# A fused attention and MLP-mixer kernel: prologue by head pairs, casting loads, column-tiled sums, and a transpose by transfer

## Chip, cores, metric

One core of one Trainium2 chip. The metric is the device time of one execution in microseconds (us). The kernel before took 424.72 us (median of 3 runs, 424.33 to 428.24) when it was first measured.

## The reference

Sliding-window attention with eight global positions, then an MLP mixer over tokens and over channels. Inputs are f32; B=8, H=8, S=576, D=64.

```python
# mask: |i-j| <= 32, or i global, or j global (8 global positions)
scores = (q @ k.T) / 8;  scores[~mask] = -1e9
attn = softmax(scores);  x = (attn @ v) as [B, 576, 512]
h  = relu(x.T @ w_tok1) @ w_tok2          # over tokens, 576 -> 256 -> 576
u  = x + h.T
out = u + relu(u @ w_ch1) @ w_ch2         # over channels, 512 -> 1536 -> 512
```

## The kernel before

Each batch has a *sparse* list of steps (transposes `T`, scores `S_`, global rows `GK`, global sums `OG`, attention times v `PV`, token mixing `M1`, `M2`, the turn of u `M3`) and a *dense* list (channel mixing `M4`, `M5`, about two thirds of TensorE's work). The dense list of batch b is merged with the sparse list of batch b+1 in proportion to given weights. Batch 0's sparse list has nothing to overlap with: it is the prologue. Batch 7's dense list is the tail. In the traces each engine works through a list of its own, and an instruction that waits holds up those behind it in this list: in the changed kernel a 0.32 us copy of POOL began at 44.19 us, behind a cast that had waited 19.12 us for its load. The list is not always in the order in which the steps are written, because steps can be moved when the program is built. So the orders below are read from traces, not from the source.

```python
def load(b):                                  # f32, tile by tile, SyncE queue
    for ti, ten in enumerate((q, k)):
        for t in range(NT):
            nc.sync.dma_start(out=n32[ti][0:n, t], in_=ten[b, :, P*t : P*t+n, :].rearrange("h p d -> p h d"))
    ...                                       # v the same way, shifted by 32 rows
def cast(b, t=None):                          # f32 -> f16 on three engines
    nc.scalar.copy(out=s["qn"][:, sl], in_=n32[0][:, sl])
    nc.vector.tensor_copy(out=s["kn"][:, sl], in_=n32[1][:, sl])
    nc.gpsimd.tensor_copy(out=vsh[b % 2][:, sl, :, 0:D], in_=n32[2][:, sl])
...
nc.scalar.dma_start(out=gidx_b, in_=bass.AP(tensor=gt32, offset=0, ap=[[0, P], [2, NG]]))   # 8 indices to 128 rows
...                                           # 16 row gathers (q, k, v) and all weight loads, issued by POOL
def OG(b):                                    # global sums: 10 matmuls over all heads
    for c in range(NT):
        for hf in range(2):
            nc.tensor.matmul(ps[:, hf, 0:4*VW], lhsT=eg[:, c], rhs=vsh[b % 2][:, c, 4*hf:4*hf+4, :], ...)
    ...                                       # 2 mask multiplications and 1 addition on DVE
def M3(b, part):                              # turn u: TensorE transposes and a DVE copy
    for i in range(2):
        for cc in range(4):
            nc.tensor.transpose(out=pu[:, i, cc, :], in_=s["u16"][:, 2*part+i, P*cc:P*cc+P], identity=ident)
    nc.vector.tensor_copy(out=s["uT"][...], in_=pu...)
...
for t in range(NT): cast(0, t)
load(1); gather_t(0); gather_t(1); globals_(0)
for _, f in sparse(0): f()
for b in range(B):
    if b + 1 < B: cast(b + 1); globals_(b + 1)
    if b + 2 < B: load(b + 2)
    merge(sparse(b + 1) if b + 1 < B else [], dense(b))
```

The softmax here doesn't subtract the row's maximum and nothing guards it: scores larger than these inputs give would overflow.

Of the kernel before, what the change touches and what calls it, by code (L numbers as in the profile page):

```python
# [15 lines left out]
P = 128  # L16
# [3 lines left out]
QS = P + NG  # L20
EW = 2 * P + NG
# [20 lines left out]
def kernel(  # L42
# [24 lines left out]
    ab = ctx.enter_context(tc.tile_pool(name="ab", bufs=2))  # L67
    pb = ctx.enter_context(tc.tile_pool(name="pb", bufs=6))
# [17 lines left out]
    n32 = [const.tile([P, NT, H, D], F32, name=f"n32_{n}") for n in "qkv"]  # L86
    nc.gpsimd.memset(n32[0][LAST:P, NT - 1], 0.0)
    nc.gpsimd.memset(n32[1][LAST:P, NT - 1], 0.0)
    nc.gpsimd.memset(n32[2][0:WIN, 0], 0.0)
    nc.gpsimd.memset(n32[2][P - WIN : P, NT - 1], 0.0)  # L90

    def load(b):
        for ti, ten in enumerate((q, k)):
            for t in range(NT):
                n = P if t < NT - 1 else LAST
                nc.sync.dma_start(
                    out=n32[ti][0:n, t], in_=ten[b, :, P * t : P * t + n, :].rearrange("h p d -> p h d")
                )
        for c in range(NT):
            r0 = WIN if c == 0 else 0  # L100
            r1 = P - WIN if c == NT - 1 else P
            j0 = P * c - WIN + r0
            nc.sync.dma_start(
                out=n32[2][r0:r1, c], in_=v[b, :, j0 : j0 + (r1 - r0), :].rearrange("h p d -> p h d")
            )

    load(0)


    gt32 = global_idx.tensor.bitcast(I32)  # L110
    gidx_b = const.tile([P, NG], I32)
    nc.scalar.dma_start(out=gidx_b, in_=bass.AP(tensor=gt32, offset=0, ap=[[0, P], [2, NG]]))
    gidx_f = const.tile([P, NG], F32)
    nc.vector.tensor_copy(out=gidx_f, in_=gidx_b)

    ident = const.tile([P, P], F16)
    make_identity(nc, ident)
    pi_i = const.tile([P, 1], I32)
    nc.gpsimd.iota(pi_i, pattern=[[1, 1]], base=0, channel_multiplier=1)

    def int_op(name, in_, s, op):
        t = const.tile([P, 1], I32, name=name)
        nc.vector.tensor_scalar(out=t, in0=in_, scalar1=s, scalar2=None, op0=op)
        return t

    def to_f(name, in_):
        t = const.tile([P, 1], F32, name=name)
        nc.vector.tensor_copy(out=t, in_=in_)
        return t

    pf = to_f("pf", pi_i)
    p8 = to_f("p8", int_op("p8i", pi_i, 3, ALU.logical_shift_right))
    p16 = to_f("p16", int_op("p16i", pi_i, 4, ALU.logical_shift_right))
    pm8 = to_f("pm8", int_op("pm8i", pi_i, 7, ALU.bitwise_and))
    pm16 = to_f("pm16", int_op("pm16i", pi_i, 15, ALU.bitwise_and))

    it_i = const.tile([P, NT * P], I32)
    nc.gpsimd.iota(it_i, pattern=[[1, NT * P]], base=0, channel_multiplier=0)
    it_f = const.tile([P, NT * P], F32)
    nc.vector.tensor_copy(out=it_f, in_=it_i)  # L140


    oh = const.tile([P, NG], F32)
    gpp = const.tile([P, 1], F32)
    nc.vector.tensor_scalar(out=oh, in0=it_f[:, 0:NG], scalar1=pm8, scalar2=None, op0=ALU.is_equal)
    nc.vector.tensor_mul(out=oh, in0=oh, in1=gidx_f)
    nc.vector.reduce_sum(out=gpp, in_=oh, axis=AX.X)


    idx_i = const.tile([P, 4 + B], I32)  # L150
    base2 = const.tile([P, 1], F32)
    nc.vector.tensor_scalar(out=base2, in0=p8, scalar1=float(2 * S), scalar2=gpp, op0=ALU.mult, op1=ALU.add)
    for t in range(2):
        for par in range(2):
            nc.vector.tensor_scalar(
                out=idx_i[:, 2 * t + par : 2 * t + par + 1], in0=base2,
                scalar1=float((32 * t + par) * S), scalar2=None, op0=ALU.add,
            )
    basev = const.tile([P, 1], F32)
    nc.vector.tensor_scalar(out=basev, in0=p16, scalar1=float(S), scalar2=gpp, op0=ALU.mult, op1=ALU.add)  # L160
    for b in range(B):
        nc.vector.tensor_scalar(
            out=idx_i[:, 4 + b : 5 + b], in0=basev, scalar1=float(b * H * S), scalar2=None, op0=ALU.add
        )


    d1 = const.tile([P, H], F32)
    d2 = const.tile([P, H], F32)
    lo8 = const.tile([P, 1], F32)
    hi8 = const.tile([P, 1], F32)  # L170
    nc.vector.tensor_scalar(out=lo8, in0=pm16, scalar1=7.5, scalar2=None, op0=ALU.is_lt)
    nc.vector.tensor_scalar(out=hi8, in0=pm16, scalar1=7.5, scalar2=None, op0=ALU.is_gt)
    nc.vector.tensor_scalar(out=d1, in0=it_f[:, 0:H], scalar1=p16, scalar2=lo8, op0=ALU.is_equal, op1=ALU.mult)
    nc.vector.tensor_scalar(out=d2, in0=it_f[:, 0:H], scalar1=p16, scalar2=hi8, op0=ALU.is_equal, op1=ALU.mult)


    mf = const.tile([P, NT * P], F16)
    onm = const.tile([P, NT * P], F16)
    nc.vector.tensor_scalar(out=mf, in0=it_f, scalar1=gpp, scalar2=lo8, op0=ALU.is_equal, op1=ALU.mult)
    nc.vector.tensor_scalar(out=onm, in0=it_f, scalar1=float(S) - 0.5, scalar2=hi8, op0=ALU.is_lt, op1=ALU.mult)  # L180
    nc.vector.tensor_add(out=mf, in0=mf, in1=onm)


    colng = const.tile([P, NT * P], F16)
    colt = const.tile([P, NT * P], F16)
    nc.vector.tensor_scalar(out=colng, in0=it_f, scalar1=float(S) - 0.5, scalar2=None, op0=ALU.is_lt)
    for g in range(NG):
        nc.vector.tensor_scalar(out=colt, in0=it_f, scalar1=gidx_f[:, g : g + 1], scalar2=None, op0=ALU.not_equal)
        nc.vector.tensor_mul(out=colng, in0=colng, in1=colt)
    bandm = const.tile([P, NT, EW - 64], F16)  # L190
    nc.gpsimd.memset(bandm, 1.0)
    rowok = const.tile([P, NT], F32)
    dk = const.tile([P, NG], F32)
    for c in range(NT):
        nc.vector.tensor_scalar(
            out=dk, in0=gidx_f, scalar1=pf, scalar2=float(-(P * c - WIN)), op0=ALU.subtract, op1=ALU.add
        )
        nc.vector.tensor_mul(out=dk, in0=dk, in1=dk)
        nc.vector.tensor_scalar(out=dk, in0=dk, scalar1=0.5, scalar2=None, op0=ALU.is_gt)
        rk = rowok[:, c : c + 1]  # L200
        nc.vector.tensor_reduce(out=rk, in_=dk, axis=AX.X, op=ALU.min)
        if c == 0:
            nc.vector.memset(rowok[0:WIN, 0:1], 0.0)
        if c == NT - 1:
            nc.vector.memset(rowok[P - WIN : P, c : c + 1], 0.0)

        left, right = bandm[:, c, 0:64], bandm[:, c, 72:200]
        nc.gpsimd.affine_select(out=left, in_=left, compare_op=ALU.is_ge, fill=0.0, base=0, pattern=[[1, 64]], channel_multiplier=-1)
        nc.gpsimd.affine_select(out=right, in_=right, compare_op=ALU.is_ge, fill=0.0, base=64, pattern=[[1, P]], channel_multiplier=-1)
        nc.gpsimd.affine_select(out=right, in_=right, compare_op=ALU.is_ge, fill=0.0, base=0, pattern=[[-1, P]], channel_multiplier=1)  # L210
        nc.vector.tensor_scalar_mul(out=bandm[:, c, :], in0=bandm[:, c, :], scalar1=rk)
        if c > 0:
            nc.vector.tensor_mul(out=left, in0=left, in1=colng[:, P * c - 64 : P * c])
        else:
            nc.vector.memset(left, 0.0)
        nc.vector.tensor_mul(out=right, in0=right, in1=colng[:, P * c : P * c + P])


    e_all = const.tile([P, H, NT, EW], F16)
    nc.vector.memset(e_all, 0.0)  # L220
    eg = const.tile([P, NT, H, 16], F16)
    nc.gpsimd.memset(eg, 0.0)
    kgz = [const.tile([P, NP, 32], F16, name=f"kgz{i}") for i in range(2)]
    vg = [const.tile([P, H, VW], F16, name=f"vg{i}") for i in range(2)]
    vsh = [const.tile([P, NT, H, VW], F16, name=f"vsh{i}") for i in range(2)]
    x16s = [const.tile([P, NT, DM], F16, name=f"x16_{i}") for i in range(2)]
    for i in range(2):
        nc.gpsimd.memset(kgz[i], 0.0)
        nc.gpsimd.memset(vg[i], 0.0)
        nc.vector.tensor_copy(out=vg[i][:, :, D : D + 1], in_=d2.unsqueeze(2))  # L230
        nc.gpsimd.memset(vsh[i][:, :, :, D + 1 : VW], 0.0)
        nc.gpsimd.memset(vsh[i][:, :, :, D : D + 1], 1.0)
    nc.gpsimd.memset(x16s[0][LAST:P, NT - 1, :], 0.0)
    nc.gpsimd.memset(x16s[1][0:LAST, NT - 1, :], 0.0)


    w1 = const.tile([P, NT - 1, DTOK], F16)
# [291 lines left out]
    def sparse(b):  # L529
# [8 lines left out]
        if b % 2:  # L538
            u += [(0.3, lambda: M3(b, 2))]
# [54 lines left out]
```

## Time and profile before

The head of the profile's page of the kernel before: busy time of each engine, then the span in 40 slices of 10.6 us (a digit is the busy share in tenths; PEclk is TensorE's granted clock).

```profile
span 422.7 us, 6930 instructions
...
PE 331.2 (78%) x2756; PEld 179.0 (42%) x2756; DVE 212.5 (50%) x434; ACT 150.0 (35%) x273; POOL 94.2 (22%) x197
...
PE   0120242678799979997999799979998999899995
...
PEclk9999999999699999999999999999999999999999
DMA  1999999996927094616660847100110021001012
```

Read the PE line from the left: nine slices of prologue in which TensorE is mostly idle, then a nearly full engine. The clock line is not to be trusted there: the first clock record of this trace comes at 81.6 us, and the global sums took 2.38 us at 71 us, as in the half-clock slice at 112 us, against 1.30 us in later batches. The stretches between the first dense matmuls (`M4`) of successive batches cut the span into parts. The columns are: stretch, its length, busy time (and instruction count) of PE, PEld, DVE, ACT, POOL, granted clock, DMA share, GB/s.

```profile
0.00:94.70 94.70, 28.45 (x245) 16.88 (x246) 47.54 (x147) 18.26 (x28) 52.38 (x105) 1.00 1.06 182
94.70:137.70 43.00, 38.96 (x303) 20.03 (x303) 21.84 (x38) 17.40 (x32) 8.04 (x16) 0.92 0.63 133
137.70:183.10 45.40, 42.23 (x376) 23.35 (x374) 23.94 (x43) 19.13 (x35) 7.85 (x16) 1.00 0.51 108
183.10:223.50 40.40, 36.99 (x319) 19.82 (x317) 23.39 (x41) 17.45 (x32) 7.60 (x16) 1.00 0.55 115
...
391.50:422.70 31.20, 26.18 (x159) 13.11 (x156) 4.20 (x7) 8.96 (x15) 0.00 (x0) 1.00 0.15 51
```

Prologue 94.7 us, seven overlapped batches 296.8 us (38.4 to 45.4 each, of which PE is busy 37 to 42), tail 31.2 us. In the prologue, TensorE's longest waits between 40 and 95 us (engine, line, releaser: total, times, longest) are these:

```profile
PE s_0_0_405 L336 <- POOL kT_0_383 L321: 16.1, 1, 16.1
PE og_528 L382 <- POOL eg L358: 10.9, 1, 10.9
```

Both end with a small instruction of POOL. The first stands in POOL's queue behind sixteen row gathers, the issue of all weight loads and batch 0's v cast, the second behind a cast of batch 1's v that waits for its load.

### The profile page before, as it was taken

The numbers are of one execution on the slowest core, as the hardware profiler recorded it, in microseconds if no ns is written. First come the engines' busy times: TensorE is split into PE (matmuls) and PEld (weight loads), VectorE is DVE, ScalarE is ACT, GpSimd is POOL, SyncE is SP. The second block draws the span as 40 slices with busy tenths as digits, with TensorE's granted clock in tenths as the row PEclk, the third lists the DMA queues.
The fourth block names the chain that finished last, engine by engine and source line by source line (L and its number), as shares of the span: only waits on it lengthen the run. The fifth ranks groups of instructions, "written<-read, shape, count | busy, mean of one in ns | idle before, by whom it ended". The sixth has DMA issues, their size and how long they took to land.

```text
span 422.7 us, 6930 instructions
## 1 busy us (share of the span) xinstructions
PE 331.2 (78%) x2756; PEld 179.0 (42%) x2756; DVE 212.5 (50%) x434; ACT 150.0 (35%) x273; POOL 94.2 (22%) x197
## 2 busy tenths in 40 slices
PE   0120242678799979997999799979998999899995
PEld 0000121444365437453645374536454745364452
DVE  4792070484545555466555653574555535556111
ACT  1202150218510772049106820392057203810520
POOL 9578842020410032003120311031201000100000
PEclk9999999999699999999999999999999999999999
DMA  1999999996927094616660847100110021001012
GB/s 25 191 207 198 205 198 215 206 189 118 187 54 173 26 170 80 163 50 124 128 161 28 140 86 186 51 0 2 51 50 3 2 76 50 2 26 50 25 47 79
DMA packets 123472, 42.48 MB, mean 101 GB/s; under 512 B 114609, under 2 KB 118577, under 8 KB 123441
## 3 DMA queue, kind: packets, MB, share of 16 engines
q1 hardware_dynamic: 112512, 28.32, 37.2%
q10 hardware_dynamic: 6288, 9.44, 6.5%
q0 software_dynamic: 4640, 4.29, 6.0%
q8 instruction: 21, 0.34, 0.3%
q14 instruction: 11, 0.08, 0.1%
HBM read 36.38 MB, written 9.44 MB: 108 GB/s over the span
## 4 chain that ended last, share of the span: by engine, by line
PE 58%; ACT 11%; DVE 11%; DMA 9%; POOL 5%; issue 4%; POOLq 0%; DVEq 0%; ACTq 0%
ACT e_all L345 4%; DVE e_all L357 3%; DMA gidx_b<-in_global_idx_dram 3%; DMA n_v<-in_v_dram 3%; ACT e_all L354 2%; ACT e_all L353 2%; DMA w_271<-in_moe_w_tok_dram 1%; DMA g_k_281<-in_k_dram,idx_i 1%; ACT e_all L352 1%; POOL eg L358 1%; DVE x_0_257 L424 1%; POOL vsh_255 L295 1%; DMA n_k<-in_k_dram 1%; PE op_4_4516 L518 1%; PE op_4_3805 L518 1%
## 5 line engine op out<-in xcount | busy, mean ns | idle before, releaser
L357 DVE TENSOR_TENSOR e_all<-e_all,bandm 128x1000 f16<-128x1000 f16 x64 | 40.8, 678 | 53.3 <-ACT e_all L354 49.9
L492 PEld LDWEIGHTS <-wc_274 128*128 128x128 f16 x384 | 34.4, 98 | 45.4 <-issue 16.2
L358 POOL COPY eg<-e_all 128x80 f16<-128x80 f16 x32 | 10.5, 327 | 81.7 <-DVE e_all L357 80.9
L412 PEld LDWEIGHTS <-e_all 128*128 128x128 f16 x320 | 24.9, 100 | 3.0 <-issue 1.7
L417 PEld LDWEIGHTS <-e_all 128*128 128x128 f16 x256 | 19.1, 101 | 1.3
L382 PEld LDWEIGHTS <-eg 128*128 128x128 f16 x80 | 8.1, 109 | 21.3 <-POOL eg L358 19.5
L295 POOL CAST vsh_256<-n_v 128x2560 f16<-128x2560 f32 x4 | 9.3, 2316 | 29.9 <-PE pv_4_1063 L412 8.6
L295 POOL CAST vsh_255<-n_v 128x512 f16<-128x512 f32 (+1 forms) x8 | 9.8, 1263 | 24.4 <-DMA n_v<-in_v_dram 9.3
L315 PE MATMUL pT_0_371<-ident,qn_322 128*128 128x128 f16 x5 | 1.4, 289 | 16.9 <-ACT qn_322 L293 16.9
L336 PE MATMUL s_0_0_405<-qT_0_382,kT_0_383 64*128 64x200 f16 x4 | 0.5, 351 | 16.1 <-POOL kT_0_383 L321 16.1
L454 PEld LDWEIGHTS <-w_273 128*128 128x128 f16 x80 | 7.8, 97 | 12.0 <-issue 3.2
L505 PEld LDWEIGHTS <-wc_274 128*128 128x128 f16 x192 | 11.1, 98 | 0.9
L382 PE MATMUL og_528<-vsh_255,eg 128*128 128x264 f16 x10 | 2.4, 425 | 10.9 <-POOL eg L358 10.9
L315 PEld LDWEIGHTS <-qn_322 128*128 128x128 f16 x20 | 1.9, 127 | 18.7 <-ACT qn_322 L293 17.7
L436 PEld LDWEIGHTS <-w_271 128*128 128x128 f16 x64 | 6.3, 99 | 7.3 <-issue 1.1
L293 ACT CAST qn_697<-n_q 128x2560 f16<-128x2560 f32 x1 | 2.3, 2324 | 18.9 <-DMA n_q<-in_q_dram 18.9
L522 DVE TENSOR_TENSOR osb_0_4465<-u_7_4235,op_0_4452 128x512 f32<-128x512 f16 x1 | 0.7, 686 | 15.1 <-PE op_0_4452 L518 15.1
L336 PEld LDWEIGHTS <-kT_0_383 64*128 64x128 f16 x10 | 0.7, 129 | 17.1 <-issue 16.1
L293 ACT CAST qn_322<-n_q 128x512 f16<-128x512 f32 x5 | 3.1, 617 | 12.7 <-DMA n_q<-in_q_dram 12.7
L315 PE MATMUL pT_0_371<-ident,kn_323 128*128 128x128 f16 x5 | 1.4, 288 | 7.4 <-DVE kn_323 L294 7.4
L518 PEld LDWEIGHTS <-b_7_4324 128*128 128x128 f16 x48 | 4.7, 98 | 5.4
L293 ACT CAST qn_1189<-n_q 128x2560 f16<-128x2560 f32 x1 | 2.3, 2325 | 12.8 <-DMA n_q<-in_q_dram 12.8
(1293 smaller groups left out, 957.5 us busy)
## 6 DMA issues: line engine op xcount, KB each, us to landing
n_q<-in_q_dram SPq DMA_DIRECT2D x32, 256.0 KB, 5.1
n_k<-in_k_dram SPq DMA_DIRECT2D x32, 256.0 KB, 5.3
n_v<-in_v_dram SPq DMA_DIRECT2D x24, 256.0 KB, 5.4
n_v<-in_v_dram SPq DMA_DIRECT2D x16, 192.0 KB, 5.0
wc_274<-in_moe_w_ch_dram POOLq DMA_DIRECT2D x3, 512.0 KB, 10.3
wc_275<-in_moe_w_ch_dram POOLq DMA_DIRECT2D x3, 512.0 KB, 17.3
n_q<-in_q_dram SPq DMA_DIRECT2D x8, 128.0 KB, 4.9
n_k<-in_k_dram SPq DMA_DIRECT2D x8, 128.0 KB, 4.8
```

Source lines behind the costliest of these rows:

```text
L295: nc.gpsimd.tensor_copy(out=vsh[b % 2][:, sl, :, 0:D], in_=n32[2][:, sl])
L345: nc.scalar.activation(out=e2[:, :, 1:3, 64:EW], in_=s1[:, :, 0:400].rearrange("p h (c x) -> p h c x", c=2), func=AF.Exp, scale=scale)
L353: nc.scalar.activation(out=e2[:, :, 4, 64 : 64 + QS], in_=s2[:, :, 136:272], func=AF.Exp, scale=scale)
L354: nc.scalar.activation(out=e2[:, :, 3, 64:EW], in_=s2[:, :, 272:472], func=AF.Exp, scale=scale)
L357: nc.vector.tensor_mul(out=eh, in0=eh, in1=bandm)
L358: nc.gpsimd.tensor_copy(out=eg[:, :, 2 * p : 2 * p + 2, 0:NG], in_=e2[:, :, :, P:QS].rearrange("p h c x -> p c h x"))
L382: nc.tensor.matmul(ps[:, hf, 0 : 4 * VW], lhsT=eg[:, c], rhs=vsh[b % 2][:, c, 4 * hf : 4 * hf + 4, :], start=(c == 0), stop=(c == NT - 1),)
L412: nc.tensor.matmul(o, lhsT=e_all[:, h, tau, QS - sh : QS - sh + P], rhs=vsh[b % 2][:, tau, h, :], start=False, stop=last and tau == NT - 1,)
L417: nc.tensor.matmul(o, lhsT=e_all[:, h, tau + 1, 0:P], rhs=vsh[b % 2][:, tau + 1, h, :], start=False, stop=last)
L492: nc.tensor.matmul(ps, lhsT=wc1[:, cc, P * j : P * j + P], rhs=s["uT"][:, cc, :], start=(cc == 0), stop=(cc == 3))
L505: nc.tensor.matmul(ps[:, i, :], lhsT=wc1[:, cc, P * j : P * j + P], rhs=s["uTl"][:, cc, :], start=(cc == 0), stop=(cc == 3),)
L518: nc.tensor.matmul(ps, lhsT=w, rhs=wc2[:, j, :], start=(j == 0), stop=(j == NJ - 1))
```

## The change

The intent: in the prologue, load batch 0 by pairs of heads so that transposes can start after a quarter of q and k, and keep batch 1's loads off POOL's and DVE's path; for batches 1 to 7, let the transfer cast f32 to f16 (POOL-issued loads), which removes three casts a batch; compute the global sums of each head pair in a 32-column tile of TensorE; build masks with fewer instructions; take v's global rows by a one-hot multiplication in place of a gather; and turn u by transfer transposes, each put right behind the product that it turns, with 3.0 of empty work at the end of the sparse list, so that the token mixing ends earlier and the transfers have time. The core of the diff:

```diff
+    for p in range(NP):                       # batch 0: by head pairs, SyncE queue, f32
+        for ti, ten in enumerate((q, k)):
+            for h in (2 * p, 2 * p + 1):
+                nc.sync.dma_start(out=n32[ti][:, 0:NT-1, h, :], in_=ten[0, h, 0:S-LAST, :].rearrange("(t p) d -> p t d", p=P))
     def load(b):                              # batches 1..7
-                nc.sync.dma_start(out=n32[ti][0:n, t], ...)
+                nc.gpsimd.dma_start(out=dst[b % 2][0:n, t], ...)      # f32 -> f16 in the transfer
 ...
     def globals_(b):
+        nc.gpsimd.tensor_copy(out=qTs[b % 2][:, :, :, 0:NG], in_=gT[:, b].unsqueeze(2).to_broadcast(...))
 ...
     def OG(b):
-            for hf in range(2):
-                nc.tensor.matmul(ps[:, hf, 0:4*VW], lhsT=eg[:, c], rhs=vsh[b % 2][:, c, 4*hf:4*hf+4, :], ...)
+            for p in range(NP):
+                nc.tensor.matmul(ps[32*p:32*p+32], lhsT=eg[:, c, 2*p:2*p+2, :], rhs=vsh[b % 2][:, c, 2*p:2*p+2, :], ...)
 ...
     def M3(b, part):
-            (8 TensorE transposes and one DVE copy)
+            for i in range(2):
+                nc.sync.dma_start_transpose(out=s["uT"][:, :, P*tau:P*tau+P], in_=s["u16"][:, tau, :])
 ...
     def sparse(b):
+        u += [(3.0, lambda: None)]
 ...
+    for p in range(NP):
+        cast0(p); T(0, p)
+        if p == 0: gather_t(0); globals_(0)
+        S_(0, p)
+    for c in range(NT): castv0(c)
+    GK(0); OG(0)
+    (load wc1, wc2);  load(1);  gather(1)      # gather(1): global rows of batches 4 to 7
+    for t in range(NT): PV(0, t)
+    M1(0); M2(0, ...) and M3(0, ...)
+    gather_t(1)
```

## The prediction

> **What bounds it now.** The span (422.7 us) has three parts (chain of waits, stretch table). Prologue, 0 to 94.7 us: PE is busy 28 us of it, DMA is full from 11 to 84 us. Seven overlapped batches, 94.7 to 391.6 (297 us; 40.5 for an even, 45.3 for an odd dense part): PE busy 37.1 and 42.1 of them, so PE-bound with 3 to 4 us of bubbles. Tail of dense work: 31 us, PE-bound.
>
> **Prologue.** In the before trace scores start at 49.8 us, released by a POOL copy that stands behind 14 indirect gathers and v casts; the global sums start at 71.2, because a POOL cast that waits for batch 1's v (DMA) stands before the copy of the global columns; PV at 74.9; dense at 94.7. The change drops batch 1's and 2's loads from that path, removes 10 gathers, moves the global columns to DVE. What stays: the 1024-element index load (12.3 us to landing), beside which the load queue hardly moves data until 11 us; 3.5 MB for batch 0 (1.18 MB took 5.8 us alone, 16 us beside the weights). In the new order on POOL the copy of the global q columns stands behind the first v cast, which stands behind all q and k and beside 4 MB of weights, so I expect scores at 32 to 38 us (estimate), the sums near 48, PV near 50. PV to dense took 19.8 us (a DVE/PE ping-pong that stays), plus 2 to 4 us for the transfer turns beside batch 1's loads. Dense starts near 72: 22 us saved.
>
> **Per batch, critical because on PE or on what PE waits for:** u's transposes go (0.98 us, 0.34 more in odd ones); column-tiled sums: 1.30 us to about 0.5 (the equally tiled row-score group takes 0.5); the score matmuls grow by 8 columns (+0.1); the q cast leaves ACT (2.33 us in the middle of the exp stretch, chain piece 0.74 and a PE wait of 0.55 and 1.0); the global copy leaves POOL (PE wait 0.6 to 0.8). DVE loses the k cast (1.5), the u copies (about 1.8), one of the row ops; it gains four small mask ops and 4% on the masks. Sum: about 3.3 us a batch; the first overlapped batch also loses a 2.8 us DMA wait. 297 becomes about 273. ACT stays the limit in the exp stretch, so some bubbles remain.
>
> **The risk is the transfer transpose.** [...] The filler of 3.0 leaves about 4 us between the last u and the first dense matmul; I expect 0 to 1 us of stall. Casting loads: [...] POOL's weight loads took 0.8 us each, so 15 a batch, estimated 1 to 1.5 us each, fit in 40 us.
>
> **Time.** 72 + 273 + 31 + 3 (stalls) = 379 us; range 360 to 398. Faster by over 2%: 0.95; within 2%: 0.02; slower: 0.03.
>
> **Right if** the chain shows dense starting at 66 to 79 us, released by DMA turns; stretches 37 to 38 and 41 to 42.5 us; PE busy about 314 us; the DMA share of the prologue still near full; POOL busy in DMA issue. **Wrong if** the first dense matmul of each batch waits over 2 us for uT; if POOL issue takes over 2.5 us a load; or if the score start is set by the pairs' loads (then near 20 us and a time near 362).

The sum is whole: 72 + 273 + 31 + 3 = 379 us. Its 3 us of stalls, and the 2 to 4 us for the transfer turns within the 72, are estimates, which no trace had shown; the 1 to 1.5 us a load is an estimate from the 0.8 us of POOL's weight loads in the trace before.

## The result

The changed kernel is correct and took 393.69 us (median of 4 runs, 393.25 to 393.81) against 424.52 us (4 runs, 422.39 to 428.24) for the kernel before on the same chip. The ratio is 0.9263, 95% interval 0.9198 to 0.9329. A ratio here is the mean time of one kernel's fast runs over the mean of the other's fast runs of the same rounds, so it is not quite the ratio of the quoted medians. The other versions' ratios are to the kernel before too.

The head of the page of the changed kernel, slices of 9.8 us:

```profile
span 391.9 us, 6622 instructions
...
PE 319.8 (82%) x2697; PEld 167.3 (43%) x2697; DVE 185.6 (47%) x400; ACT 137.2 (35%) x269; POOL 114.7 (29%) x156
...
PE   0010255659999999999999999999899999997995
...
PEclk9999999688999999999999999999999999999999
DMA  0799999991985398419853984298600041005012
```

The notches of 7 at every batch are gone from the PE line, but the prologue is nearly as long as it was. The first slice of the DMA line is new: 0. The stretches, columns as before:

```profile
0.00:87.40 87.40, 27.61 (x244) 17.21 (x245) 36.69 (x123) 14.71 (x29) 50.14 (x76) 0.94 1.20 134
87.40:125.10 37.70, 36.39 (x292) 17.69 (x293) 19.66 (x37) 14.90 (x30) 12.91 (x16) 0.95 0.87 83
125.10:166.60 41.50, 41.10 (x367) 21.94 (x368) 20.55 (x39) 17.29 (x34) 12.91 (x16) 1.00 0.83 91
166.60:203.30 36.70, 35.66 (x309) 18.02 (x307) 21.56 (x42) 15.60 (x31) 12.91 (x16) 1.00 0.92 92
...
361.00:391.90 30.90, 26.18 (x156) 13.10 (x156) 3.44 (x5) 8.96 (x15) 0.00 (x0) 1.00 0.16 53
```

| part, us | before | predicted | changed |
|---|---|---|---|
| first dense matmul | 94.7 | 72 | 87.35 |
| seven overlapped stretches | 296.8 | 273 | 273.6 |
| tail | 31.2 | 31 | 30.95 |

Odd dense parts took 43.8 to 45.4 us and now take 41.4 or 41.5; even ones took 38.4 to 43.0 and now take 36.7 to 37.8. Predicted were 41 to 42.5 and 37 to 38. The prologue gained 7 us where 22 were predicted. The list of the longest waits before 95 us, changed kernel, with those of TensorE and the POOL and DVE waits that bear on them:

```profile
PE pT_0_266 L347 <- ACT qn_79 L328: 23.1, 1, 23.1
...
POOL vsh_83 L336 <- DMA n_v<-in_v_dram: 19.1, 1, 19.1
...
PE s_0_0_288 L364 <- POOL qT_168 L339: 14.5, 1, 14.5
...
DVE kn_81 L328 <- DMA n_k<-in_k_dram: 9.2, 4, 6.0
```

The first is TensorE standing idle from the start of the span until the first pair of q heads is there and cast. The third says that the scores still start with a POOL copy. POOL's timeline shows why (columns: start, duration, engine, line, operation; in brackets the idle time before it and its releaser):

```profile
41.54 1.91 POOL L336 CAST vsh_83<-n_v 32x512 f16<-32x512 f32 x3 [19.12 <-DMA n_v<-in_v_dram]
43.39 0.75 POOL L221 DMA_DIRECT2D wc_185<-in_moe_w_ch_dram  x1
44.19 0.32 POOL L339 COPY qT_168<-gT 128x160 f16<-128x160 f16 x1
...
44.56 0.53 PE L364 MATMUL s_0_0_288<-qT_168,kT_170 64*128 64x208 f16 x4 [14.53 <-POOL qT_168 L339]
```

A 0.32 us copy of batch 0's global columns stands behind a v cast that waited 19 us for its load. In the source the copy (`globals_(0)`) is written before the v casts and before the loads of `wc1` and `wc2`; on POOL it ran behind the first v cast and behind five of those six loads. An edit can therefore also change orders that it does not name. Where the steps of batch 0 begin:

| us | scores | sums | PV | M2 | first dense |
|---|---|---|---|---|---|
| before | 49.8 | 71.2 | 74.9 | 88.6 | 94.7 |
| changed | 44.6 | 58.6 | 61.2 | 77.7 | 87.35 |

So the theory to test was: the steady part is understood in sum, and the prologue loses 15 us to an index load, to orders within POOL's and DVE's queues, and to the transfer turn. The rival: the prologue is limited by the volume of loads and would not move with any of them.

### The profile page after: what moved, and what is told of

The parts are those of the page before. It is cut to its first block, busy times and chain, and to the rows that moved or that the text cites. A ratio compares the mean times of both kernels' runs of the same rounds, so it can differ in the third digit from the quotient of the medians.

```text
span 391.9 us, 6622 instructions
## 1 busy us (share of the span) xinstructions
PE 319.8 (82%) x2697; PEld 167.3 (43%) x2697; DVE 185.6 (47%) x400; ACT 137.2 (35%) x269; POOL 114.7 (29%) x156
## 3 DMA queue, kind: packets, MB, share of 16 engines
q1 hardware_dynamic: 33776, 8.26, 11.2%
## 4 chain that ended last, share of the span: by engine, by line
PE 59%; ACT 9%; DMA 3%; DVE 1%; SPq 1%; issue 1%; ACTq 0%
ACT e_all L374 2%; ACT e_all L383 2%; ACT e_all L382 1%; ACT e_all L381 1%; SPq L498 1%; DMA out_dram<-osb_0_2979 1%; DMA uT_3972<-u_7_3940 1%; PE op_4_4213 L535 1%; PE op_2_3013 L535 1%; PE op_2_2030 L535 1%; PE op_2_1047 L535 1%; PE op_2_3981 L535 1%; PE op_0_2938 L535 1%; PE op_0_3463 L535 1%; PE op_3_4197 L535 1%
## 5 line engine op out<-in xcount | busy, mean ns | idle before, releaser
L509 PEld LDWEIGHTS <-wc_184 128*128 128x128 f16 x384 | 33.0, 98 | 45.1 <-issue 15.8
L390 DVE TENSOR_TENSOR e_all<-e_all,bandm 128x1040 f16<-128x1040 f16 x64 | 42.4, 704 | 0.5
L123 POOL DMA_DIRECT2D qn_80<-in_q_dram x20 | 17.5, 873 | 60.6 <-PE pT_3_1738 L347 22.8
L123 POOL DMA_DIRECT2D qn_79<-in_q_dram x15 | 13.2, 883 | 40.2 <-PE pT_3_1217 L347 20.1
L384 DVE TENSOR_TENSOR eg<-e_all,bandm 128x160 f16<-128x160 f16 x32 | 7.7, 242 | 31.0 <-ACT e_all L383 31.0
L128 POOL DMA_DIRECT2D vsh_84<-in_v_dram x20 | 16.9, 865 | 14.4 <-PE pv_2_916 L444 1.5
L347 PE MATMUL pT_0_266<-ident,qn_79 128*128 128x128 f16 x5 | 0.7, 309 | 23.1 <-ACT qn_79 L328 23.1
L347 PEld LDWEIGHTS <-qn_79 128*128 128x128 f16 x80 | 6.1, 106 | 28.4 <-ACT qn_79 L328 23.1
L364 PEld LDWEIGHTS <-kT_170 64*128 64x128 f16 x160 | 6.2, 103 | 27.4 <-issue 13.8
L123 POOL DMA_DIRECT2D kn_82<-in_k_dram x20 | 17.6, 878 | 0.0
L128 POOL DMA_DIRECT2D vsh_83<-in_v_dram x15 | 12.7, 881 | 9.6 <-PE b1lp_0_1385 L522 1.1
L328 ACT CAST qn_79<-n_q 64x128 f16<-64x128 f32 (+1 forms) x8 | 3.4, 456 | 32.8 <-DMA n_q<-in_q_dram 32.8
L481 PEld LDWEIGHTS <-w_183 128*128 128x128 f16 x80 | 8.2, 103 | 12.6 <-issue 4.8
L123 POOL DMA_DIRECT2D kn_81<-in_k_dram x15 | 13.3, 888 | 0.0
L336 POOL CAST vsh_83<-n_v 32x512 f16<-32x512 f32 (+1 forms) x9 | 6.2, 697 | 19.3 <-DMA n_v<-in_v_dram 19.1
L522 PEld LDWEIGHTS <-wc_184 128*128 128x128 f16 x192 | 11.1, 98 | 0.6
L364 PEld LDWEIGHTS <-kT_171 64*128 64x128 f16 x160 | 5.2, 95 | 12.8 <-issue 8.5
L463 PEld LDWEIGHTS <-w_181 128*128 128x128 f16 x64 | 6.3, 101 | 6.4 <-issue 1.9
```

The costliest lines, as they stand in the source:

```text
L123: nc.gpsimd.dma_start(out=dst[b % 2][0:n, t], in_=ten[b, :, P * t : P * t + n, :].rearrange("h p d -> p h d"))
L128: nc.gpsimd.dma_start(out=vsh[b % 2][r0:r1, c, :, 0:D], in_=v[b, :, j0 : j0 + (r1 - r0), :].rearrange("h p d -> p h d"),)
L364: nc.tensor.matmul(ps[:, par, off : off + n], lhsT=kT[r, P * c : P * c + P], rhs=qf[r, lo : lo + n], start=True, stop=True,)
L390: nc.vector.tensor_mul(out=eh, in0=eh, in1=bandm)
L481: nc.tensor.matmul(ps[:, i, :], lhsT=w2[:, ch, P * tau - sh : P * tau - sh + P], rhs=s["a1"][:, ch, :], start=(ch == 0), stop=(ch == 1),)
L509: nc.tensor.matmul(ps, lhsT=wc1[:, cc, P * j : P * j + P], rhs=s["uT"][:, cc, :], start=(cc == 0), stop=(cc == 3))
```

## Experiments

Each version is the changed kernel with the edit shown or named, and all gave correct results. "First dense" is the start of batch 0's first dense matmul in the profiled run.

### e1_rows: the index load with longer pieces

`gidx_b` brings eight 4-byte values, each from a separate address, to each of 128 rows: 1,024 pieces of 4 bytes.

```diff
-    gidx_b = const.tile([P, NG], I32)
+    gidx_b = const.tile([P, NG, 2], I32)      # both halves of the 64-bit indices: 128 rows of 64 contiguous bytes
-    ... ap=[[0, P], [2, NG]]
+    ... ap=[[0, P], [1, 2 * NG]]
-    nc.vector.tensor_copy(out=gidx_f, in_=gidx_b)
+    nc.vector.tensor_copy(out=gidx_f, in_=gidx_b[:, :, 0])
```

> One edit of the changed kernel: the index list comes as 128 rows of 64 contiguous bytes instead of 1024 elements of 4 bytes. In the changed kernel's trace the element load runs at about 105 packets a us and no other transfer moves from 3 to 12 us. Theory A (that load holds back every transfer, and the prologue is set by when q, k and v of batch 0 land): other transfers move from about 3 us on, the first pair's q is cast before 15 us (22.4 now), scores start 7 to 9 us earlier than 44.6, the first dense matmul is at 78 to 81 us (87.35 now), the time 385 to 388 us. Rival B (the prologue is set later, by batch 1's loads and the turn transfers, or the total of transfers is the limit in any case): scores start earlier but the first dense matmul moves by less than 3 us and the time stays at 391 to 394 us.

Measured: 387.05 us (386.92 to 387.79), ratio 0.912 (0.9083 to 0.9157); scores at 36.8, first dense at 80.26 in place of 87.35. Packets begun per 2 us, counted in the trace's DMA records:

```
us          changed: index  bulk (SyncE)  POOL      e1_rows: index  bulk  POOL
2 to 4               186        528         0                 144    431     0
4 to 6               212          0         0                 104    111    52
6 to 8               212          0         0                  40    428   391
8 to 10              174          0         0                   0    724   288
10 to 12             209          0         0                   0   1695    90
12 to 14             145         69       104                   0   1533    67
```

What follows: in the changed kernel some 105 four-byte packets a microsecond moved and, from 4 to 12 us, nothing else on any queue (the expectation says from 3 us, but bulk packets began until 3.9 us). With 128 longer pieces the load landed 5.9 us after its issue, not 14.4, and the whole kernel gained 6.6 us. The kernel before has the same load (12.3 us to landing; no bulk packet began there from 7.8 to 11.2 us), so this is a cost that the change kept.

### e2_cols: the global columns of batch 0 copied by DVE

```diff
     def globals_(b):
-        nc.gpsimd.tensor_copy(
+        (nc.vector if b == 0 else nc.gpsimd).tensor_copy(
```

> One edit: in batch 0 alone the copy of the global q columns runs on DVE, right after the columns are made, instead of on POOL behind the first v cast. Theory A (POOL's order, which sent the scores behind all of q, k and the first v, is a real cost of the prologue): scores start at about 37.5 us instead of 44.6, and the first dense matmul and the time come 4 to 7 us earlier (387 to 390). Rival B (the global sums need all of v cast anyway, which ends at 50.5 us, and the four pairs land until 40.5 us): scores start at 37.5 but the sums move by under 3 us and the time stays within 2 us of 393.7.

Measured: 394.6 us (393.45 to 395.0), ratio 0.9295 (0.9253 to 0.9337): no gain. But the scores started at 37.7, 6.9 us earlier, as the POOL reading said. M2 started at 77.6, as without the edit. Most of the time was taken back between PV and M2 (21.6 us in place of 16.5), by a DVE that waits for global rows gathered for batches 4 to 7 (lines of DVE's and TensorE's waits from 40 to 80 us):

```profile
DVE g_q L311 <- DMA g_q<-in_q_dram,idx_i: 4.6, 1, 4.6
...
DVE g_k L311 <- DMA g_k<-in_k_dram,idx_i: 2.2, 1, 2.2
...
PE pv L431 <- DVE x L451: 8.4, 4, 6.2
```

That gather is issued by POOL behind batch 1's fifteen casting loads. The casts of its rows stand in DVE's queue in the middle of the normalisations of PV (although `gather_t(1)` is written behind all of them), and PV waits for those. In the changed kernel itself DVE had waited there 2.2 us only, because the scores were late.

### e3_both: e1_rows and e2_cols together

> Both edits of the two kernels before. Theory A (the two waits stand one behind the other on one chain): the gains add up, 11 to 15 us, time 379 to 383 us, about what was predicted for the change. Rival B (they are two ways to the same limit, the landing of v or of batch 1): no better than the better of the two by more than 2 us.

Measured: 389.15 us (386.88 to 392.24), ratio 0.9153 (0.9098 to 0.9207), not distinguishable from e1_rows alone. Scores at 21.4, 23 us earlier than in the changed kernel; sums at 45.8, 13 us earlier; M2 at 70.1, against 70.5 in e1_rows. Two things swallowed the gain. Against e1_rows the scores came 15.4 us earlier but the sums only 5.1. Between them ACT and DVE waited for the later pairs' loads: on ACT, pair 0's exp stood behind the q cast of the last pair, and DVE waited 10.4 us for k.

```profile
28.45 0.62 ACT L328 CAST qn<-n_q 128x512 f16<-128x512 f32 x1 [10.53 <-DMA n_q<-in_q_dram]
28.97 0.86 ACT L374 ACTIVATE e_all<-s 128x832 f16<-128x832 f32 x1
```

Most of what was left went into the wait of e2_cols (4.9 and 2.2 us on DVE; TensorE's `pv` waited 9.5 us, 7.2 at once).

### e12_all: and the second gather issued early

```diff
     gather(0)
+    gather(1)
 ...
     load(1)
-    gather(1)
```

(on top of e3_both)

> e3_both and one more edit: the second set of row gathers (batches 4 to 7) is issued directly behind the first set, not behind batch 1's fifteen casting loads. Theory A: in e3_both the gain of 23 us at the score start was lost because the DVE casts of the second gather stand in the middle of DVE's PV stretch and wait for DMA (4.9 and 2.2 us of wait); with the gather early those waits go, the second dense part of the token mixing (M2) starts at 60 to 65 us in place of 70.1, the first dense matmul at 70 to 76 in place of 79.4, time 380 to 384 us. Rival B: the PV stretch is held by something else (weights w1 and w2 that land late, or the half TensorE clock), then M2 still starts at 68 to 71 and the time stays 387 to 390.

Measured: 382.29 us (381.89 to 386.18), ratio 0.9001 (0.8919 to 0.9082); M2 at 60.1, first dense at 74.2. The expectation of theory A held in each number: the waits for `g_q` and `g_k` (7.1 us) are gone, and M2 came 10.0 us earlier. But the edit did more than remove them. The scores started at 28.5, 7.1 us later than in e3_both: DVE's mask steps, which stand before the main k cast of batch 0's first pair, waited for a mask step of POOL that now comes behind the four extra gathers. The stretch from scores to sums then took 14.3 us in place of 24.4, and the sums came 2.9 us earlier (lines of DVE's waits to 75 us, then of TensorE's from 55 to 80 us):

```profile
DVE bandm L288 <- POOL band L279: 6.1, 1, 6.1
```

On TensorE a new wait stands out:

```profile
PE b1p L510 <- DMA uT<-u: 8.6, 1, 8.6
PE hp L482 <- DMA qn<-in_q_dram: 1.0, 1, 1.0
```

### e11_late: the early second gather alone

> The changed kernel with one edit alone: the second set of row gathers is issued directly behind the first. Theory A: it takes the 2.2 us of DVE wait out of the PV stretch, but the scores still start at 43 to 45 us (index load and POOL order are as they were), so the first dense matmul comes about 2 to 7 us earlier than the 87.35 us of the changed kernel: 387 to 391.5 us. Alone it must be worth less or no more than the 7 us that it gave on top of the other two edits. Rival B: the gather competes with batch 0's loads for the DMA queues and delays the scores by as much as it saves later: 392 to 395 us.

Measured: 393.13 us (392.78 to 393.34), ratio 0.9237 (0.9168 to 0.9307): the same as the changed kernel within the intervals. In the profiled run the first dense matmul did come 2.7 us earlier (84.7), but later stretches were 1.8 us longer in sum. The time lies in the range of the rival, whose reason did not occur here: the scores started at 42.8, not later (on top of the other two edits they did start later, see e12_all). What is shown is that this edit is worth about nothing alone, and 6.9 us (389.15 to 382.29; the profiled first dense moved 5.2 us) on top of the other two.

### e13_order: transposes one pair ahead in the prologue

```diff
-    for p in range(NP): cast0(p); T(0, p); ...; S_(0, p)
+    (pairs 0 and 1: cast0, T)  S_(0, 0)  (pair 2)  S_(0, 1)  (pair 3)  S_(0, 2)  S_(0, 3)
```

(on top of e12_all)

> The version with all three waits removed, and in the prologue the transposes of pair p+1 put ahead of the scores of pair p (two pairs of transposes, then scores and transposes in turn), as every later batch has it. Theory A: the score stretch of 14.3 us (28.5 to 42.9) is a serial ping-pong of transposes, copies and scores over two PSUM buffers; it shrinks by 2 to 4 us and the time to 378 to 380.5 us. Rival B: the stretch is bound by ScalarE's exp and DVE's masks, or PV waits for the v casts anyway: 381.5 to 383.5 us.

Measured: 383.85 us (382.55 to 384.79), ratio 0.9007 (0.8937 to 0.9078): no gain. The score stretch did shrink, from 14.3 to 10.4 us, so the serial reading of it was right. But the last v cast was not ready and PV started at 45.0 in place of 45.8:

```profile
38.96 0.90 PE L413 MATMUL og<-vsh,eg 128*32 128x132 f16 x16 [0.31 <-ACT e_all L384]
41.90 1.90 POOL L337 CAST vsh<-n_v 32x512 f16<-32x512 f32 x3 [3.75 <-DMA n_v<-in_v_dram]
43.85 0.30 PE L413 MATMUL og<-vsh,eg 128*32 128x132 f16 x4 [3.99 <-POOL vsh L337]
```

So a wait for v's loads took back most of the gain, as the rival said. Of the 0.9 us that were left at M2 (59.2) nothing reached the first dense matmul (74.6 in place of 74.2): from M2 to there it took 15.4 us, against 14.1, with the transfer turn in between. The order was not tried again with that turn out of the way, so what it is worth there stays open.

### e4_peturn: u turned on TensorE again, in all batches

```diff
     def M3(b, part):
-        nc.sync.dma_start_transpose(...)
+        (8 TensorE transposes into PSUM and one DVE copy, as before the change)
```

> One part of the change undone: u is turned by TensorE and DVE again, with the schedule (the turn right behind its product, the filler of 3.0) kept. In the changed kernel the turn of batch 0 takes from 80.8 (u ready) to 87.35 us; TensorE did the same in 2.7 us in the kernel before. Theory A (the transfer turn saves TensorE time in the overlapped batches and costs latency once in the prologue): the prologue gets 3 to 4 us shorter, each of the seven overlapped batches 0.9 to 1.5 us longer, time 396 to 400 us. Rival B (the overlapped batches have bubbles that absorb the turns): batches longer by under 0.4 us each, time at or below 392 us.

Measured: 392.64 us (391.71 to 393.52), ratio 0.9254 (0.9212 to 0.9296): no difference from the changed kernel. The first dense came 2.6 us earlier; the seven stretches were 274.5 us in sum against 273.6 (odd ones 0.9 us longer, even ones not). In these stretches TensorE was busy 271.9 us against 266.1, so the transfer turn did save it 5.8 us. But it was idle 2.6 us against 7.6: in the changed kernel it waited for `uT` before every odd batch's dense part, 4.8 us in sum, and these waits are gone.

```profile
PE b1p_0_4022 L509 <- DMA uT_3972<-u_7_3940: 2.0, 1, 2.0
PE b1p_0_3083 L509 <- DMA uT_3004<-u_5_2972: 1.3, 1, 1.3
PE b1p_0_1117 L509 <- DMA uT_1038<-u_1_1006: 0.8, 1, 0.8
PE b1p_0_2100 L509 <- DMA uT_2021<-u_3_1989: 0.7, 1, 0.7
```

### e15_turn0: batch 0's u turned on TensorE, the others by transfer

On top of e12_all; the edit is that of e4_peturn behind `if b == 0`.

> The version with all three waits removed, and batch 0's u turned on TensorE (16 transposes, two DVE copies); all other batches keep the transfer transposes. Theory A: the 8.6 us for which the first dense matmul waited for uT are the transfer's own time beside batch 1's casting loads, so the first dense matmul comes 4 to 6 us earlier (68 to 70.5 us), time 376.5 to 379 us. Rival B: the first dense matmul would wait then for a channel weight (wc1) or for the half clock of TensorE: earlier by under 2 us, 380.5 to 382.5 us.

Measured: **372.43 us** (371.13 to 375.45), ratio 0.8773 (0.8696 to 0.885). This is the best version; its interval lies wholly below that of the changed kernel. The first dense matmul starts at 65.6, 8.6 us earlier than in e12_all. The gain was larger than expected. From e12_all's and then e15_turn0's timeline:

```profile
62.41 5.73 SPq L499 DMA_TRANSPOSE uT<-u  x4
...
74.22 3.57 PE L510 MATMUL b1p<-uT,wc 128*128 128x512 f16 x8 [8.60 <-DMA uT<-u]
```

```profile
62.20 0.62 PE L501 MATMUL pu<-ident,u 128*128 128x128 f16 x8 [0.45 <-DVE u L487]
63.19 0.68 DVE L504 COPY uT<-pu 128x1024 f16<-128x1024 f16 x1
63.92 0.61 PE L501 MATMUL pu<-ident,u 128*128 128x128 f16 x8
64.79 0.67 DVE L504 COPY uT<-pu 128x1024 f16<-128x1024 f16 x1
...
65.62 1.89 PE L522 MATMUL b1p<-uT,wc 128*128 128x512 f16 x8
```

The four transfers' packets ran from 64.6 to 73.3 us in e12_all, with casting loads interleaved all the while. By their place in POOL's queue these are batch 2's, not batch 1's as the expectation has it. In the changed kernel, where batch 2's loads ended at about 84 us, the packets ran from 82.3 to 86.9. The fix of the earlier waits had moved the turn into the loads. Whether later loads of batch 2 would have served as well as the turn on TensorE was not tried. The half clock went too: TensorE's clock lines, e12_all and then e15_turn0 (slices of 9.5 and 9.2 us):

```profile
PEclk9999999689999999999999999999999999999999
```

```profile
PEclk9999999999999999999999999999999999999998
```

The first stretch is 36.5 us in e15_turn0 and 38.5 in e12_all, so about 2 us more came back after the wait itself. In e12_all's trace the half clock ran from 68.7 to 78.9 us, and began inside the gap of 8.6 us (65.6 to 74.2). In the changed kernel half clock from 87.8 to 91.3 followed a wait of 2.8 us that ended at 87.35. How long a gap has to be for this was not measured.

### e8_nofill and e17_peturn_nofill: a square of turn and empty work

```diff
-        u += [(3.0, lambda: None)]
```

(e8_nofill: the changed kernel; e17_peturn_nofill: e4_peturn)

> The changed kernel with the 3.0 of empty work at the end of the sparse list taken out, so that the last token-mixing matmuls come later, close to the next batch's first dense matmul. Theory A: the transfer transposes take 3 to 6 us from u to uT and the filler hides them; without it each of the seven batches waits 2 to 4 us, 407 to 420 us. Rival B: the transfers are short enough (below 2 us), at most 0.5 us a batch, 393 to 397 us.

> The changed kernel with all turns of u on TensorE and without the 3.0 of empty work: the fourth corner of a square (transfer turn with empty work 393.7 us, without it 413.5; TensorE turn with it 392.6). Theory A: the empty work is needed only to hide the transfer; a TensorE turn needs little lead, so this version loses at most 3 us against the one with it: 392 to 396 us. Then the transfer with its filler together bought almost nothing. Rival B: the empty work helps by itself, because the end of the token mixing is a chain of TensorE and DVE steps whose bubbles are better filled when it ends earlier: 1 to 2 us in each of seven batches, 399 to 407 us.

| median, us (ratio, interval) | with empty work | without |
|---|---|---|
| transfer turn | 393.69 (0.9263, 0.9198 to 0.9329) | 413.54 (0.9709, 0.9633 to 0.9786) |
| TensorE turn | 392.64 (0.9254, 0.9212 to 0.9296) | 392.89 (0.9249, 0.9214 to 0.9284) |

Without its empty work the transfer turn costs 20 us. The seven stretches are 19.7 us longer: TensorE is idle in them for 23.5 us in place of 7.6, and busy for 3.9 us more, with four stretches of half clock of 3.4 us each that follow such waits (mean granted clock of the profiled run 0.977, changed kernel 0.982). The idle time is mostly these two lines of e8_nofill's waits from 87 to 380 us (13.4 and 6.3 us, where the changed kernel waited 4.8 for `uT`):

```profile
PE b1p L509 <- DMA uT<-u: 13.4, 5, 3.3
PE b1p L509 <- issue: 6.3, 2, 3.7
```

With a TensorE turn the empty work makes no difference. So the transfer turn and its filler together bought nothing measurable in the changed kernel: the filler repairs what the transfer costs. Theory A of both runs held.

### e5_ogfull and e6_f32loads: the two other parts undone

e5_ogfull: the global sums by ten full matmuls again. e6_f32loads: batches 1 to 7 loaded as f32 on the SyncE queue and cast on ScalarE, DVE and POOL again (q's f32 buffer gets a place of its own for it).

> The changed kernel with one part undone: the global sums are again ten full-width matmuls (four heads each) and two mask multiplications, no column tiling. Theory A: the column tiling saves 0.6 us of TensorE per batch and TensorE bounds the overlapped batches, so the stretches grow by about 0.6 us each, 4 to 5 us in all: 397 to 399 us. Rival B: the sums fall into a bubble (the stretch waits for ScalarE there), 393 to 395 us.

> The changed kernel with one part undone: loads of batches 1 to 7 come as f32 on the SyncE queue and are cast by ScalarE (q), DVE (k) and POOL (v), as before the change. Theory A: the casts stood in the exp stretch and in front of the transposes, and their removal is the largest part of the steady gain of 23 us: stretches grow by 1.5 to 2.2 us each, 404 to 409 us. Rival B: the casts were off the critical path, at most 0.5 us a batch, 393 to 397 us.

Measured: e5_ogfull 397.4 us (396.56 to 397.88), ratio 0.9325 (0.9257 to 0.9393); seven stretches 277.4 us, 3.8 more than the changed kernel. e6_f32loads 401.01 us, the median of its three fast runs (399.21 to 403.68; a slow one took 408.57), ratio 0.9393 (0.9303 to 0.9483); seven stretches 284.1 us in the profile, 10.5 more, with the first dense at 87.0, much as in the changed kernel; TensorE's waits for `uT` there are 5.2 us against 4.8, so they are not what grew. So the casting loads are the largest single part of the steady gain that was isolated, a little below the range expected in the time, and the column tiling is worth what was expected: the sums themselves went from 1.30 to 0.70 us a batch, and the stretches lost 0.54. Both intervals overlap the changed kernel's (0.9198 to 0.9329), so the stretches of the profiled runs are the firmer evidence.

## Why the prediction was right or wrong

**The verdict** (faster, 379 us, range 360 to 398) held; the median was 14.7 us above the point. The difference adds up: 15.35 for the prologue, 0.6 for the stretches, 3 us of stalls that were added but lie inside the stretches and so come off (4.8 us of waits for `uT` were measured there), and 1.8 between span and time.

**The steady part was right, and right for mostly the stated reasons.** 273 us predicted, 273.6 measured. The casts' share (10.5 us in seven stretches) and the sums' share (3.8) were isolated. The turn's share was predicted as "u's transposes go (0.98 us, 0.34 more in odd ones)" and came to 0.9 us in all seven together: TensorE saved 5.8 us of work and waited 4.8 us for `uT` instead. So that the sum came within 0.6 us of the prediction is partly luck: a gain forecast for the turn was made up by terms that were not isolated. Of the 23.2 us that the stretches lost, about 8 are left for parts that were not undone singly (the global copies, the mask and row ops, the 2.8 us DMA wait of the first stretch); effects of single undoings need not add, so that split stays open.

**"scores at 32 to 38 us (estimate)" failed: 44.6 measured.** The prediction did see both terms, the index load and the copy behind the v cast. It put them in as a range and not as costs. The runs sized them: e1_rows brought the start to 36.8, e2_cols to 37.7, both to 21.4. Each alone would have fulfilled the step.

**"PV to dense took 19.8 us …, plus 2 to 4 us for the transfer turns" failed: 26.1 measured.** From PV to M2 it took 2.8 us longer than before, from M2 to first dense 3.6. The second is within the 2 to 4 us that were allowed for the turn. The first was missing: the gather for batches 4 to 7, moved behind batch 1's loads, put a DMA wait (2.2 us) into DVE's PV stretch, which the prediction did not have at all; it grew to 6.8 and 7.1 us as the scores came earlier, which is why e2_cols gained nothing. The turn became dear only later: from M2 to first dense it took 6.1 us before the change, 9.6 in the changed kernel, 14.1 in e12_all and 5.8 in e15_turn0. The whole PV to dense took 19.4 us in e15_turn0, close to the 19.8 of before.

**The prologue, added up** (first dense matmul, each line the step from the version above it): changed 87.35; index rows −7.1 (80.26); columns on DVE −0.9 (79.38); early gather −5.2 (74.22); TensorE turn of batch 0 −8.6 (65.62). With the first three, the kernel reaches what was predicted for the change as it stands: dense at 74 and 382 us, against 72 and 379. The rival theory, that the volume of loads sets the prologue whatever is edited, is refuted by the 21.7 us; that single stretches of it wait for loads is seen in e3_both and e13_order.

**The transfer transpose** was the named risk. The prediction allowed for 16 blocks of 128x128 in series and a long stall in each batch; this was the estimate. This case shows 128x512 per instruction, issued every 1.2 to 1.3 us, landing 2.4 us after issue in the median. Four turns, 16 blocks, took 4.5 us of packets in batch 0 of the changed kernel (6.0 us from the first issue to the last packet), with casting loads beside them for the first 1.6 us, and 8.7 us of packets in e12_all, with casting loads beside them throughout. Whether single blocks go in series was not shown; a long stall in each batch did not occur. The risk came in by another door: time beside casting loads in the prologue once the earlier waits were gone, and the need of a filler later. A last wait for `uT` of 0.7 to 2.0 us stayed before every odd batch, where 0 to 1 us was expected.

**The gathers** were counted loosely: sixteen became eight, of which four stand before the scores. **POOL's issue** was estimated at 1 to 1.5 us a load. It took 0.86 to 0.89 us in the mean. The fifteen loads of a batch, with one copy of 0.4 us, occupy POOL 12.9 us of a stretch, off the critical path except in the prologue.

**PE busy** came to 319.8, not about 314; 316.5 in e15_turn0, which has no half clock from 60 to 366 us, so part of the excess is slow clock and not work.

## What to carry to other kernels

In a prologue, follow each engine's queue in the order that the trace shows, not only the data: here a 0.3 us copy stood behind a cast that waited 19 us, a gather for batch 4 delayed batch 0, and removing one such wait exposed the next, so two fixes (the early gather, and the turn on TensorE) measured as worthless singly and gained 7 and 10 us in the right company (the second then for batch 0 alone). Measure a transfer transpose against the plain TensorE version. Here the transfer needed empty work to hide (413.54 us without it, 393.69 with it), and the packets of four turns took 8.7 us with casting loads beside them throughout, against 4.5 us with such loads for the first 1.6 us only; the TensorE version was as fast over the steady part (274.5 us against 273.6) and brought the first dense matmul 8.6 us earlier in the prologue of e15_turn0. Bring small index tables in contiguous rows: in the changed kernel 1,024 4-byte pieces held up every other load for 8 us (4 to 12 us), and 128 rows of 64 bytes in their place made the kernel 6.6 us faster.
